# Two one-bank PSUM tiles in place of a two-bank one from the last batch on, and a planner that counts the landing between dependent transfers

## The chip, the cores and the metric

The kernel runs on one core of one Trainium2 chip. The metric is device time in microseconds of one execution, lower is better; for the kernel before three runs are given, and their median is what the prediction is about. One further execution was profiled, and all rows below come from it.

## What is computed

Attention between 2,048 tokens and a small state (8 heads of 64, four sequences of 512 tokens with 32 state rows), then two MLPs on the 2,176 rows that come out of it:

```python
def _moe_ref(x, w_in, w_out):
    h = x @ w_in                          # (2176, 512) @ (512, 2048)
    neg, pos = h <= -1.0, h >= 1.0
    g = np.where(pos, h, np.where(neg, 0.0, (h + 1.0) ** 2 / 4.0))
    return g @ w_out                      # (2048, 512)

def _moe2_ref(x, w_a, w_b, w_out):        # 512 -> 1536 -> 512
    return (x @ w_a) * (x @ w_b) @ w_out
```

The weights arrive in double precision; the result is single precision.

## The kernel before, in words

**Precision.** A matrix product in single precision is made of three matmuls on a high and a low half of each operand (`three`, L376). The halves are made by a *split* (`split`, L357): ScalarE copies the value to the rounded format (L345, the high half), VectorE subtracts it (L355, the low half).

**Fewer products.** The large products use a seven-product scheme on 2 x 2 blocks. Its products are named "1" to "7", and `sums` (L776) says what happens to each result in its PSUM bank: products 1, 5, 6 and 4 are copied out by ScalarE (`copy`, L781, an ACTIVATE `f<-bank` on L345), products 2, 3 and 7 are added by VectorE (`add`, L784). Three banks take part, x, y and z (`TO`, L797): 1, 6, 7 and 4 go to x, 2 goes to y, 5 and 3 to z. Products 3, 6, 7 and 4 add onto what the bank holds, so product 3 begins only after bank z has been copied for product 5, and product 6 only after bank x has been copied for product 1.

**Stages.** (1) Attention and the first MLP's input layer run interleaved (`phase_one`, L1250), in four batches of 16 units. A unit (`h_mm`, L721) is six matmuls of 512 columns into one bank, followed by `gate`. The first three batches take banks 0 to 3 in turn; attention takes banks 4 and 5 for scores and 6 and 7 for the rest. From unit 48 on (`SWITCH`), the last batch, units take banks 4, 5, 6, 7, 2, 3 in turn, since attention is done; its third unit, number 50, is the first on bank 6. The first products of stage 2 are mixed into this batch. (2) `b_steps` (L870) is the first MLP's output layer, in three chunks of 2 x 368, 2 x 368 and 2 x 352 tokens. Each product has four inner blocks and two column halves m; in every block six matmuls go to the first bank of a pair and six to the second (L918 to L931). Product 5 and product 3 use banks 6 and 7 as that pair (`bz`, L856); products 1, 6, 7 and 4 use banks 0 and 1 or 2 and 3; product 2 uses 4 and 5. (3) `ab_run` (L1049) makes the second MLP's two input layers and multiplies them: six pairs of inner blocks, three token chunks each; a product is six matmuls, and the rows `p` are stored to DRAM in four pieces per chunk (L1086 to L1093). Meanwhile the third weight matrix is converted and put into DRAM (`u_conv`, L1367). Conversions (`conv_steps`, L389) are a weight load (L400), a byte copy on ScalarE (L420), another ScalarE pass (L345) and a VectorE step (L433). (4) `o_plain` (L1168) and eight times `o_run` (L1185) make the output from `p`. A run loads 256 tokens of `p` in two loads (L1187), and a product is 18 matmuls of 256 columns. The first run's products 1, 5, 2, 6, 3 are followed by the second run's product 1. The buffers of the runs' loads lie where stage 3 kept its result rows, so the load of the second run waits until the last of those rows have been stored.

**PSUM tiles.** Banks 0 to 5 are six tiles of one bank each; banks 6 and 7 are the two halves of one tile of 1,024 columns (L450 to L452).

**The order.** Nothing is ordered by hand. Each operation is recorded by `Flow.op` (L46) with what it reads and writes, and `Flow.order` (L85) simulates the engines and writes the instructions in the order of the simulated starts. TensorE's order is fixed, but for a few loose attention operations. The other engines take whatever is ready first, by due time among what is ready at once. On the chip every engine, and SP's queue of transfers, works strictly in that written order. Dependences through DRAM are kept by cells of 32 columns (`GRAIN`, L27), and PSUM by bank. A transfer's landing is reckoned as the wire time of its bytes plus a latency; for all other dependences between operations of one engine the follower may start when the engine is free (L178):

```python
DMA_RATE = 390e3
DMA_LAT = 2.2
...
fin[i] = free[e] + self.LAT[e]
if ops[i][3]:
    wire = max(wire, free[e]) + ops[i][3] / self.DMA_RATE
    fin[i] = wire + self.DMA_LAT
for s in after[i]:
    left[s] -= 1
    when[s] = max(when[s], free[e] if (e,) == (*ops[s][0],) else fin[i])
```

All transfers belong to the one engine SP, so two transfers that depend on each other are such a pair. The lines that do the transfers are L333 (`load`), L336 (`store`) and L400 (weights).

Of the kernel before, what the change touches and what calls it, by code (L numbers as in the profile page):

```python
# [9 lines left out]
F32 = mybir.dt.float32  # L10
# [5 lines left out]
PSUM = bass.MemoryType.PSUM  # L16
# [3 lines left out]
class Flow:  # L20
# [64 lines left out]
    def order(self):  # L85
        ops = self.ops
        n = len(ops)
        after = [[] for _ in range(n)]
        for i, (_, _, deps, _) in enumerate(ops):
            for d in deps:  # L90
                after[d].append(i)
        least = [min(e.values()) for e, _, _, _ in ops]

        est, pe = [0.0] * n, 0.0
        for i, (e, _, deps, size) in enumerate(ops):
            t = max((est[d] for d in deps), default=0.0)
            if "PE" in e:
                t = pe = max(pe, t) + least[i]
            else:
                t += least[i] + (self.DMA_LAT + size / self.DMA_RATE if size else 0)  # L100
            est[i] = t + 0.1

        late, pe = [0.0] * n, None
        ideal, t = {}, 0.0
        for i, (e, _, _, _) in enumerate(ops):
            if "PE" in e:
                if i not in self.loose:
                    ideal[i] = t
                t += least[i]
        for i in range(n - 1, -1, -1):  # L110
            e, _, _, size = ops[i]
            lat = self.LAT[next(iter(e))]
            x = min((late[s] for s in after[i]), default=est[i] + 12.0)
            took = least[i] + lat + (self.DMA_LAT + size / self.DMA_RATE if size else 0)
            late[i] = x - took
            if i in ideal:
                late[i] = min(late[i], ideal[i])
        late = [x - self.hurry[i] for i, x in enumerate(late)]
        free = dict.fromkeys(self.LAT, 0.0)
        ready = {e: [] for e in free}  # L120
        left = [len(d) for _, _, d, _ in ops]
        when, fin, start = [0.0] * n, [0.0] * n, [None] * n
        chain = [i for i in range(n) if "PE" in ops[i][0] and i not in self.loose]
        at, lag, wire = 0, 0.0, self.DMA_FROM
        shared = {"DVE": 0.0, "POOL": 0.0}

        def offer(i):
            for e in ops[i][0]:
                if e != "PE" or i in self.loose:
                    ready[e].append(i)  # L130

        for i in range(n):
            if not left[i]:
                offer(i)
        for _ in range(n):
            best = None
            for e, f in free.items():
                x = None
                if e == "PE" and at < len(chain) and not left[chain[at]]:
                    i = chain[at]  # L140
                    x = (max(f, when[i]), 1e9, i, e)
                soon = min((max(f, when[i]) for i in ready[e]), default=0.0)
                soon += self.SOON if soon < self.EARLY else 0.0

                z = None
                for i in ready[e]:
                    t = max(f, when[i])
                    if t <= soon:
                        y = (late[i], t, i)
                        z = min(z, y) if z else y  # L150
                if z:
                    y = (z[1], z[0], z[2], e)
                    x = min(x, y) if x else y
                if x:
                    best = min(best, x) if best else x
            if best is None:

                raise RuntimeError("nothing is ready")
            t, _, i, e = best
            start[i] = t  # L160
            free[e] = t + ops[i][0][e]
            if i in self.port and e in shared:
                other = shared["POOL" if e == "DVE" else "DVE"]
                free[e] += min(max(other - t, 0.0), ops[i][0][e])
                shared[e] = free[e]
            if i in ideal:
                at += 1
                lag = max(lag, t - ideal[i])
            else:
                for x in ops[i][0]:  # L170
                    ready[x].remove(i)
# [3 lines that stand above are left out]
                fin[i] = wire + self.DMA_LAT  # L175
            for s in after[i]:
                left[s] -= 1
                when[s] = max(when[s], free[e] if (e,) == (*ops[s][0],) else fin[i])  # L178
                if not left[s]:
                    offer(s)  # L180
            self.ops[i] = (*ops[i][:4], e)
        self.start, self.fin, self.lag, self.late = start, fin, lag, late
        return sorted(range(n), key=lambda i: (start[i], i))
# [3 lines left out]
def attention_then_two_mlps(  # L187
# [14 lines left out]
    P = 128  # L202
# [13 lines left out]
    SWITCH = 48  # L216
# [18 lines left out]
    flow = Flow()  # L235
    op = flow.op
# [26 lines left out]
    class V2:  # L263
# [18 lines left out]
        @property  # L282
        def regs(self):
            a = BASE[self.arena] + self.at
            return [("S", a + 4 * self.step * i, a + 4 * (self.step * i + self.n)) for i in range(self.k)]
# [17 lines left out]
    def bank(b):  # L303
        return ("P", b, b + 1)
# [23 lines left out]
    def t_mm(n, passes=1):  # L328
        return passes * max(n / 2400 + 0.0135, 0.112)
# [30 lines left out]
        hi_of(hi, src, n, regs(src), regs(hi) + list(also))  # L360
        tt(lo, src, lambda: hi(F32), ALU.subtract, n, regs(src, hi), regs(lo))

    def mms(b, cols, pairs, first, last, n, rd, onto=False, off=0):


        def emit(e):
            o = banks[b][:, off : off + cols]
            for k, (w, x) in enumerate(pairs()):

                nc.tensor.matmul(  # L370
                    o, w, x, start=first and k == 0, stop=last and k == n - 1, skip_group_check=onto
                )

        return op({"PE": n * t_mm(cols)}, emit, rd, [bank(b)])

    def three(w, x):  # L376

# [67 lines left out]
    ps = ctx.enter_context(tc.tile_pool(name="ps", bufs=1, space=PSUM))  # L445
# [2 lines left out]
    arenas["R0"] = pc.tile([P, RLO // 4], F32R, name="r0")  # L448
    arenas["F0"] = pc.tile([P, F0 // 4], F32, name="f0")
    banks = [ps.tile([P, 512], F32, name=f"bank{b}") for b in range(6)]  # L450
    upper = ps.tile([P, 1024], F32, name="bank67")
    banks += [upper[:, :512], upper[:, 512:]]  # L452
    spare = pc.tile([P, 1], F32, name="spare")
    g_d = pd.tile([F1, P, T], F32, name="g_d")
    x2_d = pd.tile([4, P, T], F32, name="x2_d")
# [236 lines left out]
    four, six = Ring([0, 1, 2, 3]), Ring([4, 5, 6, 7, 2, 3] * 2 + [6, 7, 2, 3])  # L692

    begun = {}
    units, first_w = [], []

    def gate(b, g, put):
        h = lambda: banks[b]
# [22 lines left out]
    def h_mm(j, f, cs=range(2)):  # L721
        b = begun.pop((j, f)) if cs[0] else (four if 16 * j + f < SWITCH else six)()
        n, o = divmod(f, 4)

        def pairs():
            out = []
            for q in cs:
                out += three([v()[:, P * o : P * o + P] for v in wsum[n][q]], [v() for v in att[2 * j + q]])
            return out

        used = [v.sub(P * o, P) for q in cs for v in wsum[n][q]] + [v for q in cs for v in att[2 * j + q]]
        units.append(mms(b, 512, pairs, cs[0] == 0, cs[-1] == 1, 3 * len(cs), regs(*used)))
        if cs[-1] < 1:
            begun[j, f] = b
            return
        g = (qring if 16 * j + f < SWITCH else qlast)()
        here = [dram("G", f, S * j, S * j + S)]
        gate(b, g, lambda: store(lambda: g_d[f, :, S * j : S * j + S], g, here, 1 << 18))
# [635 lines left out]
    for fp in range(F2 // 2):  # L1374
        for c in range(3):
            more = fp + 1 < F2 // 2
            s = 2 * fp + 2
# [21 lines left out]
    cols, end = o_plain()  # L1399
# [19 lines left out]
    with tc.manual_schedule():  # L1419
        nc.vector.memset(half, 0.5)  # L1420
        nc.scalar.activation(spare, half, AF.Exp)
        make_identity(nc, ident)
        pool = tc.tile_pool(name="fs", bufs=1)
        arenas["FS"] = pool.__enter__().tile([P, FSB // 4], F32, name="fs")
        for i in order:
            if i == first_rh[0]:
                pool.__exit__(None, None, None)
                del arenas["FS"]
                high = tc.tile_pool(name="rh", bufs=1)
                arenas["RH"] = high.__enter__().tile([P, (R0 - RLO) // 4], F32R, name="rh")  # L1430
                pool = tc.tile_pool(name="f1", bufs=1)
                arenas["F1"] = pool.__enter__().tile([P, F1B // 4], F32, name="f1")
            if i == first_r1[0]:
                pool.__exit__(None, None, None)
                del arenas["F1"]
                pool = tc.tile_pool(name="r1", bufs=1)
                arenas["R1"] = pool.__enter__().tile([P, F1B // 4], F32R, name="r1")
            flow.ops[i][1](flow.ops[i][4])
        pool.__exit__(None, None, None)
        high.__exit__(None, None, None)  # L1440


# [46 lines left out]
```

## Time and profile before

| | us |
|---|---|
| three runs | 732.38, 734.49, 733.77 |
| median | 733.77 |
| the profiled execution | 731.92 |
| its span, first to last instruction | 729.8 |
| TensorE busy in the span | 703.7 |
| VectorE busy | 560.1 |
| ScalarE busy | 426.1 |
| GpSimd busy | 106.8 |

PE is TensorE's matmuls, PEld its weight loads, DVE VectorE, ACT ScalarE, POOL GpSimd, SP the queue that issues the transfers. A row of the timeline tells start, duration, engine, line, operation, out<-in with tile names, and how many instructions it merges; in brackets stands how long the engine sat idle before it and what ended that. A row of waits tells the total of such idle time, how often it came and the longest. The chain is what ended last, followed back step by step. TensorE's granted clock was 0.998 of full speed over the span. Ends of matmuls are modelled, so their starts are the safer numbers.

### The profile page before, as it was taken

The page shows a single profiled execution, that of the slowest core. Times are in us where ns is not written, and L with a number is a line of the kernel's source. Part 1 is how long each engine was busy: PE and PEld are TensorE (multiplying, and loading weights), DVE is VectorE, ACT ScalarE, POOL GpSimd, SP SyncE. Part 2 cuts the span into 40 slices and gives each one's busy share as a digit, 9 for nine tenths or more (in the row PEclk, how much of TensorE's full clock was granted, in tenths as well). Part 3 has the DMA queues.
Part 4 walks back from the last instruction along what each step waited for, and adds up shares of the span by engine and source line. Part 5 has one row for each costly group of instructions (what it writes and reads, how often), then busy time and mean ns, then how long its engine had stood idle before and what let it go on. Part 6 is the DMA issues. An engine that isn't in the chain of part 4 may idle for free.

```text
span 729.8 us, 12347 instructions
## 1 busy us (share of the span) xinstructions
PE 703.7 (96%) x4818; PEld 655.8 (90%) x4818; DVE 560.1 (77%) x750; ACT 426.1 (58%) x651; POOL 106.8 (15%) x84
## 2 busy tenths in 40 slices
PE   8789999999999999999999999999999998999997
PEld 6445766889999999999999999999999998999997
DVE  6887878889897597789898786765636787986760
ACT  4887898788444445656566675655425445544440
POOL 3546676675000000000000000000000000000000
PEclk9999999999999999999999999999999999999999
DMA  9958788495666147134335757454541258354201
GB/s 346 384 187 244 263 283 277 146 343 180 221 199 234 38 134 236 50 104 170 90 127 164 261 185 244 149 177 141 186 154 40 87 158 283 102 179 138 82 37 43
DMA packets 75450, 128.92 MB, mean 177 GB/s; under 512 B 5632, under 2 KB 51200, under 8 KB 75392
## 3 DMA queue, kind: packets, MB, share of 16 engines
q1 hardware_dynamic: 75392, 128.15, 52.7%
q8 instruction: 37, 0.61, 0.4%
q14 instruction: 21, 0.17, 0.1%
HBM read 84.87 MB, written 43.25 MB: 176 GB/s over the span
## 4 chain that ended last, share of the span: by engine, by line
PE 79%; DVE 7%; DMA 6%; ACT 4%; issue 2%; POOL 1%; POOLq 0%; ACTq 0%; SPq 0%; DVEq 0%
PE bank L370 74%; DMA f<-in_w_dram 3%; PE bank L747 2%; ACT f L345 2%; DVE rh L355 1%; DMA p_d<-f 1%; DMA g_d<-fs 1%; DVE r L355 1%; PE bank L594 1%; DVE f L822 1%; DVE f L433 1%; PE bank L771 1%; DVE f L355 1%; DMA f<-p_d 1%; ACT r L345 1%
## 5 line engine op out<-in xcount | busy, mean ns | idle before, releaser
L370 PE MATMUL bank<-rh,r 128*128 128x352 f32 (+2 forms) x1398 | 224.6, 316 | 4.5 <-ACT f L345 3.8
L370 PEld LDWEIGHTS bank<-rh,r 128*128 128x128 f32 x1398 | 215.6, 189 | 7.7 <-ACT f L345 5.9
L370 PE MATMUL bank<-r,r 128*128 128x368 f32 (+1 forms) x960 | 156.6, 315 | 3.3 <-ACT f L345 3.2
L345 ACT ACTIVATE f<-bank 128x368 f32<-128x368 f32 (+3 forms) x183 | 82.3, 454 | 121.3 <-PE bank L370 120.6
L370 PEld LDWEIGHTS bank<-r,r 128*128 128x128 f32 x960 | 147.8, 188 | 4.1 <-ACT f L345 4.1
L345 ACT ACTIVATE rh<-f 128x736 fp32r<-128x736 f32 (+4 forms) x120 | 100.7, 847 | 80.8 <-PE bank L370 63.9
L355 DVE TENSOR_TENSOR rh<-f,rh 128x736 fp32r<-128x736 f32 (+5 forms) x120 | 118.3, 996 | 31.2 <-ACT rh L345 30.9
L355 DVE TENSOR_TENSOR f<-bank,f 128x368 f32<-128x368 f32 (+2 forms) x168 | 85.7, 517 | 71.3 <-PE bank L370 66.3
L370 PE MATMUL bank<-r 128*128 128x512 f32 (+1 forms) x582 | 121.7, 360 | 1.9 <-DVE r L355 1.2
L370 PEld LDWEIGHTS bank<-r 128*128 128x128 f32 x582 | 94.3, 189 | 28.9 <-issue 5.9
L355 DVE TENSOR_TENSOR r<-f,r 128x768 fp32r<-128x768 f32 (+6 forms) x85 | 95.8, 1137 | 21.4 <-ACT r L345 21.3
L345 ACT ACTIVATE r<-f 128x768 fp32r<-128x768 f32 (+6 forms) x85 | 80.3, 953 | 45.1 <-PE bank L370 18.3
L370 PE MATMUL bank<-rh 128*128 128x352 f32 (+2 forms) x564 | 93.3, 318 | 0.5 <-DVE f L355 0.5
L822 DVE TENSOR_TENSOR f<-f 128x256 f32<-128x256 f32 (+7 forms) x108 | 87.1, 824 | 5.1 <-issue 3.2
L370 PEld LDWEIGHTS bank<-rh 128*128 128x128 f32 x564 | 88.4, 189 | 1.5 <-issue 0.7
L370 PE MATMUL bank<-r,rh 128*128 128x368 f32 (+1 forms) x480 | 80.6, 315 | 0.4 <-DVE rh L355 0.4
L370 PEld LDWEIGHTS bank<-r,rh 128*128 128x128 f32 x480 | 74.2, 188 | 0.7 <-DVE rh L355 0.7
L420 ACT ACTIVATE f<-f 128x512 fp8e5<-128x512 fp8e5 (+1 forms) x31 | 32.3, 1043 | 29.7 <-DMA f<-in_w_dram 21.2
L345 ACT ACTIVATE f<-f 128x1024 fp8e5<-128x1024 f32 (+1 forms) x43 | 48.1, 1121 | 1.8 <-POOL f L422 1.6
L433 DVE SCALAR_TENSOR_TENSOR f<-f 128x1024 uint32<-128x1024 uint32 (+1 forms) x34 | 35.4, 1041 | 7.6 <-ACT f L345 7.5
L715 DVE SCALAR_TENSOR_TENSOR f<-f,bank 128x512 f32<-128x512 f32 x40 | 26.5, 680 | 8.2 <-POOL f L710 5.1
L710 POOL TENSOR_TENSOR f<-f 128x512 f32<-128x512 f32 x23 | 29.9, 1303 | 19.2 <-ACT f L701 19.0
(55 smaller groups left out, 440.8 us busy)
## 6 DMA issues: line engine op xcount, KB each, us to landing
f<-in_w_dram SPq DMA_DIRECT2D x25, 1024.0 KB, 7.1
f<-g_d SPq DMA_DIRECT2D x36, 368.0 KB, 4.7
f<-p_d SPq DMA_DIRECT2D x17, 768.0 KB, 4.8
g_d<-f SPq DMA_DIRECT2D x40, 256.0 KB, 4.6
f<-in_w_dram SPq DMA_DIRECT2D x18, 512.0 KB, 3.9
p_d<-f SPq DMA_DIRECT2D x48, 184.0 KB, 2.1
g_d<-fs SPq DMA_DIRECT2D x28, 256.0 KB, 4.9
f<-g_d SPq DMA_DIRECT2D x16, 352.0 KB, 4.5
```

Source lines behind the costliest of these rows:

```text
L345: lambda e: nc.scalar.activation(dst(), src(), func, **{k: (v() if callable(v) else v) for k, v in kws.items()}),
L355: op({"DVE": t_tt(n)}, lambda e: nc.vector.tensor_tensor(dst(), a(), b(), alu), rd, wr, port=port)
L370: nc.tensor.matmul(o, w, x, start=first and k == 0, stop=last and k == n - 1, skip_group_check=onto)
L420: nc.scalar.activation(to(), of(), AF.Copy, saturate=False)
L433: lambda e: nc.vector.scalar_tensor_tensor(out(U32), words_of(1, U32)(), 5, z(U32), ALU.logical_shift_right, ALU.bitwise_or),
L594: nc.tensor.matmul(banks[ab[q]][o : o + NS, :cols].rearrange("p (f x) -> p f x", x=P), st[q]()[64 * h : 64 * h + 64, NS * j : NS * j + NS] ...
L710: eng(e).tensor_tensor(g(), g(), g(), ALU.mult)
L715: lambda e: nc.vector.scalar_tensor_tensor(g(), g(), 1.0, h(), ALU.min, ALU.max),
L747: nc.tensor.matmul(banks[b][:, P * i : P * i + P], w[:, P * c : P * c + P], xs()[:, P * c : P * c + P], start=c == 0, stop=c == 3,)
L771: nc.tensor.matmul(banks[3][:, :128], ident, ident, start=True, stop=True)
L822: lambda e: eng(e).tensor_tensor(dst(), a(), b(), alu),
```

## The change

Three things are changed. Banks 6 and 7 stay one tile of 1,024 columns up to the last batch's third unit, the first on bank 6. There that tile's pool is closed and two tiles of one bank each take its place for the rest of the kernel. That unit is recorded as writing both banks, so it waits until both have been read. And in `Flow.order` an operation that depends on a transfer may start only when the transfer has landed, also where it is itself a transfer.

```diff
@@ Flow.order
-                when[s] = max(when[s], free[e] if (e,) == (*ops[s][0],) else fin[i])
+                when[s] = max(when[s], free[e] if (e,) == (*ops[s][0],) and not ops[i][3] else fin[i])
@@ mms
-    def mms(b, cols, pairs, first, last, n, rd, onto=False, off=0):
+    def mms(b, cols, pairs, first, last, n, rd, onto=False, off=0, also=()):
...
-        return op({"PE": n * t_mm(cols)}, emit, rd, [bank(b)])
+        return op({"PE": n * t_mm(cols)}, emit, rd, [bank(b), *also])
@@ the PSUM tiles
     banks = [ps.tile([P, 512], F32, name=f"bank{b}") for b in range(6)]
-    upper = ps.tile([P, 1024], F32, name="bank67")
-    banks += [upper[:, :512], upper[:, 512:]]
+    banks += [None] * 2
+    wide = {}
@@ h_mm
-        units.append(mms(b, 512, pairs, cs[0] == 0, cs[-1] == 1, 3 * len(cs), regs(*used)))
+        also = ()
+        if 16 * j + f == SWITCH + 2:
+            also = [("P", 6, 8)]
+            narrow.append(len(flow.ops))
+        units.append(mms(b, 512, pairs, cs[0] == 0, cs[-1] == 1, 3 * len(cs), regs(*used), also=also))
@@ where the order is written out
+        both_banks = tc.tile_pool(name="pw", bufs=1, space=PSUM)
+        opened = both_banks.__enter__()
+        for name, b in (('upper', 6),):
+            wide[name] = opened.tile([P, 1024], F32, name=name)
+            banks[b : b + 2] = [wide[name][:, :512], wide[name][:, 512:]]
...
         for i in order:
+            if i == narrow[0]:
+                both_banks.__exit__(None, None, None)
+                both_banks = tc.tile_pool(name="pn", bufs=1, space=PSUM)
+                opened = both_banks.__enter__()
+                banks[6:] = [opened.tile([P, 512], F32, name=f"bank{b}") for b in range(6, 8)]
```

## Rows read from the trace of the kernel before

**Rows 1.** The page's busy line: us, share of the span, instructions.

```profile
PE 703.7 (96%) x4818; PEld 655.8 (90%) x4818; DVE 560.1 (77%) x750; ACT 426.1 (58%) x651; POOL 106.8 (15%) x84
```

**Rows 2.** Stretches: us; busy PE, PEld, DVE, ACT, POOL; clock, DMA share, GB/s.

```profile
196.00:250.00 54.00, 54.00 (x322) 53.78 (x322) 41.87 (x45) 24.70 (x34) 0.00 (x0) 1.00 0.49 167
...
313.00:334.00 21.00, 21.00 (x131) 21.00 (x131) 19.37 (x19) 13.05 (x19) 0.00 (x0) 1.00 0.55 177
...
392.00:450.00 58.00, 57.99 (x351) 57.99 (x352) 44.51 (x71) 39.03 (x57) 0.00 (x0) 1.00 0.67 218
```

**Rows 3.** TensorE's costliest wait: waiter <- releaser, us in total, times, longest.

```profile
PE bank L370 <- ACT f L345: 7.0, 8, 3.2
```

**Rows 4.** Timeline of TensorE, stage 2, chunk 1.

```profile
235.31 8.21 PE L370 MATMUL bank<-rh 128*128 128x368 f32 x48
243.36 8.21 PE L370 MATMUL bank<-rh,r 128*128 128x368 f32 x48
252.14 1.27 PE L370 MATMUL bank<-rh,r 128*128 128x368 f32 x6 [0.57 <-ACT f L345]
253.98 6.31 PE L370 MATMUL bank<-rh,r 128*128 128x368 f32 x36 [0.57 <-ACT f L345]
```

**Rows 5.** Timeline of ScalarE, chunk 1: copies of product 5, split, of product 6.

```profile
251.61 0.48 ACT L345 ACTIVATE f<-bank 128x368 f32<-128x368 f32 x1 [1.20 <-PE bank L370]
253.45 0.48 ACT L345 ACTIVATE f<-bank 128x368 f32<-128x368 f32 x1 [1.36 <-PE bank L370]
...
263.40 0.82 ACT L345 ACTIVATE rh<-f 128x736 fp32r<-128x736 f32 x1 [1.20 <-PE bank L370]
...
268.38 0.48 ACT L345 ACTIVATE f<-bank 128x368 f32<-128x368 f32 x1 [0.18 <-PE bank L370]
269.38 0.48 ACT L345 ACTIVATE f<-bank 128x368 f32<-128x368 f32 x1 [0.53 <-PE bank L370]
```

**Rows 6.** Timeline of TensorE, stage 2, chunk 2.

```profile
304.53 5.91 PE L370 MATMUL bank<-rh,r 128*128 128x352 f32 x35 [0.60 <-DVE rh L355]
310.99 1.24 PE L370 MATMUL bank<-rh,r 128*128 128x352 f32 x6 [0.55 <-ACT f L345]
312.79 22.51 PE L370 MATMUL bank<-rh,r 128*128 128x352 f32 x138 [0.55 <-ACT f L345]
```

**Rows 7.** Timeline of TensorE, stage 4, first run: products 5, 2 and 6.

```profile
604.63 2.29 PE L370 MATMUL bank<-r,rh 128*128 128x256 f32 x18
606.75 2.29 PE L370 MATMUL bank<-r,r 128*128 128x256 f32 x18
612.25 0.97 PE L370 MATMUL bank<-r,r 128*128 128x256 f32 x6 [3.20 <-ACT f L345]
```

**Rows 8.** The chain before: start, us, what; last store, then load.

```profile
601.30 4.92 DMA p_d<-f
...
606.37 4.69 DMA f<-p_d
```

**Rows 9.** Timeline of ScalarE and VectorE there: split, copy, low half.

```profile
611.08 0.84 ACT L345 ACTIVATE r<-f 128x768 fp32r<-128x768 f32 x1 [5.04 <-DMA f<-p_d]
611.83 0.36 ACT L345 ACTIVATE f<-bank 128x256 f32<-128x256 f32 x1
611.95 0.96 DVE L355 TENSOR_TENSOR r<-f,r 128x768 fp32r<-128x768 f32 x1 [3.68 <-ACT r L345]
```

**Rows 10.** The chain before the stall at 304.53 us: its first split.

```profile
285.67 0.76 ACT rh L345
```

**Rows 11.** Timeline: last reads of banks 6 and 7; last batch's start.

```profile
137.86 1.28 DVE L355 TENSOR_TENSOR r<-bank,r 128x512 fp32r<-128x512 f32 x2
...
147.05 5.28 PE L370 MATMUL bank<-r 128*128 128x512 f32 x22
```

**Rows 12.** Timeline of ScalarE, stage 4's first split.

```profile
577.39 1.49 ACT L345 ACTIVATE r<-f 128x1536 fp32r<-128x1536 f32 x1 [1.13 <-DMA f<-p_d]
```

**Rows 13.** Waits from 392 to 585 us: conversions waiting for weight loads.

```profile
ACT f L420 <- DMA f<-in_w_dram: 7.7, 8, 1.6
```

More of the change, by code (lines that the diff above doesn't have):

```diff
@@ L694, in attention_then_two_mlps @@
     begun = {}
-    units, first_w = [], []
+    units, first_w, narrow = [], [], []
     def gate(b, g, put):
@@ L1440, in attention_then_two_mlps @@
         high.__exit__(None, None, None)
+        both_banks.__exit__(None, None, None)
 def kernel(**inputs):
```

## The prediction

> **What bounds the kernel now.** First the page's busy line: TensorE is busy 96% of the span, and no other engine is near it [rows 1]. The profiled execution took 731.92 us, its span 729.8 us, so 2.1 us lie around the span. The median of the three runs, 733.77 us, is 1.85 us above that execution; what I take off comes from the one execution, and I take it off the median. Next the stages: from 196 to 250 us and from 392 to 450 us TensorE does not pause at all [rows 2]. In such a kernel a microsecond comes back only where TensorE waits, and only if the engines that feed it have the work ready that much earlier. So the third view is the one that counts: who ended TensorE's waits. Its costliest line is one kind, matmuls waiting for ScalarE copies of a bank, 7.0 us in eight waits, the longest 3.2 us [rows 3]. Six are pairs of about 0.55 us, one pair in each of the three token chunks of the second stage (chunks 1 and 2 in [rows 4, 6]; chunk 0 has the same pair, six waits in all). One is the 3.2 us at 612 us [rows 7]. The eighth, in the last run, is on a bank of the lower six, where the change alters nothing, so I leave it.
>
> **The six waits: the PSUM half.** In each chunk product 5 ends with six matmuls into bank 6, then six into bank 7; ScalarE copies both banks; product 3 then adds onto bank 6, then bank 7. Bank 6 is complete one group before bank 7, so its copy could run beside the six matmuls into bank 7. The trace shows that it does not. The two copies start at 251.61 and 253.45 us, 1.84 us apart, each after the whole of TensorE's work so far [rows 5], and after each TensorE waits 0.57 us [rows 4]. For comparison: after product 6 the banks 2 and 3 are copied, and product 7 adds onto both at once, the same pattern on two tiles of one bank each. Those copies start at 268.38 and 269.38 us, 1.00 us apart [rows 5], and the timeline has no wait of TensorE there. I read the difference as the two-bank tile: a copy out of one half waits for the matmuls into the other.
>
> The idle column gives 4 x 0.57 + 2 x 0.55 = 3.4 us. Matmul ends are modelled, so I price by starts instead. An undisturbed block of 48 matmuls takes 243.36 - 235.31 = 8.05 us, six take 1.01 [rows 4]. The block at 243.36 us is followed at 252.14, after 8.78 us: 0.73 lost. The six at 252.14 are followed at 253.98, after 1.84 us: 0.83 lost. That is 1.56 us a chunk; chunk 2, with 352 columns, has 1.80 us between its two starts [rows 6] against 0.96 (1.01 x 352 / 368), 0.84 lost, and I give its first wait chunk 1's 0.73. Together 3 x 1.56 = **4.7 us**, with 3.4 us as the lower bound.
>
> The page shows 96% for matmuls and 90% for weight loads [rows 1], so the two measures of one engine differ by 6% of the span. [...] By the idle column both halves of the change could give 3.4 + 3.2 = 6.6 us, by starts 8.1 us.
>
> Once the halves are two tiles the cover is there: bank 6's copy (0.48 us) lies beside six matmuls (1.0 us), bank 7's copy beside the next six. Does TensorE keep the time? In those stretches ScalarE's splits wait for TensorE, by 1.2 us each [rows 5], so the feed moves with it. The next stall, 0.60 us at 304.53 us on VectorE splits [rows 6], goes back to a ScalarE split at 285.67 us that TensorE itself had released [rows 10], and should only move earlier.
>
> The edge that makes the batch's third unit wait for both banks, and the swap of the tiles there, I cost at nothing: the last read of those banks before the batch ends at 139.1 us (137.86 + 1.28), and TensorE starts the batch at 147.05 us with two other units ahead of the third [rows 11], so close to 8 us or more cover it. If that cover were gone, the price would be the wait itself. In the last batch proper TensorE does not wait, so the narrower tiles gain nothing there.
>
> **The 3.2 us wait: the planner half.** The old planner lets a load start, in its reckoning, when the store it depends on has been issued. At 601.30 us the last product rows are stored from a buffer that the next load overwrites; the load is really issued at 606.37 us, 4.92 us after the store began, and lands 4.69 us later [rows 8]. ScalarE's queue has that load's split ahead of the copy of bank 0, so ScalarE sits idle 5.04 us until 611.08, and the copy comes at 611.83 [rows 9]. TensorE, which needs the copied bank for product 6, starts at 612.25 us; the two products before it start 2.12 us apart, so it should have started at 606.75 + 2.12 = 608.9. Lost: **3.4 us** [rows 7].
>
> The new rule moves the planned landing later by the store's own transfer and latency: by the planner's constants 0.5 + 2.2 us, used here for order alone. The first run's copies after products 1 and 5 are ready one product apart, so the split goes behind the first copy for sure and about level with the second. Behind both, all 3.4 us come back. Between them TensorE stalls one product later instead: the second copy could not begin before the split ends near 611.8, product 3 would start at about 612.25 instead of 611.0, and 2.1 us come back. Then the data: the second run's first product is due at 608.9 + 2 x 2.12 = 613.1; its low half ends on VectorE at 611.95 + 0.96 = 612.9 [rows 9]. That fits with 0.2 us to spare, and another 0.96 us operation ahead of it on VectorE would cost 0.7 us. I take 3.0 us, nearer the upper bound because VectorE too should no longer stand behind a late load just before; bounds 0 and 3.4.
>
> What else moves: in chunks 0 and 1 of each pair of inner blocks the second store of each row shares a 32-column cell with the first (368 is not a multiple of 32), so the planner now issues it after the first one's landing. Weight loads, and the stores of the third weight matrix, can pass it on SP's queue. Nobody reads those rows before the last stage, whose first split (577.39 us [rows 12]) is needed when that stage's matmuls begin: 72 of 256 columns at 2.12 / 18 us and one product of stage 3 at 1.0 us lie before 602.5 us [rows 7], so near 593 us. The split's two halves, 1.5 us and about as much again, leave more than 10 us of cover; beyond that each microsecond would go straight to TensorE. The loads of the third weight matrix also start later in the plan; they have the same cover.
>
> **Sum.** 4.7 + 3.0 = 7.7 us: 733.77 - 7.7 = **726.1 us**.
>
> **Rivals.** *A: only the PSUM half pays.* The split stays ahead of the copies, or the second run's first product waits for its data instead. For it: the planner allows 2.7 us for a store that took 4.9, and the margin above is 0.2 us. Against: VectorE's work before it moves up too. 733.77 - 4.7 = 729.1 us. *B: the six waits are real.* Product 3 adds onto the bank that product 5 left, so it must wait for that bank's copy. The rows of banks 2 and 3 speak against it [rows 5]. If it holds, only the planner half is left: 733.77 - 3.4 = 730.4 us. [...] *C: VectorE becomes the bound.* It is busy 19.37 of 21 us from 313 to 334 us [rows 2]; what chunks 0 and 1 save (3.1 us) would come back as a longer stall at 304.53 us. 733.77 - 7.7 + 3.1 = 729.2 us. *D, slower: a weight conversion ahead of the copies.* Every later plan time shifts, and ScalarE is in order. From 392 to 585 us conversions wait eight times for weight loads, 7.7 us in all, up to 1.6 us [rows 13], today without harm, since two products (2.0 us) run between a copy and the matmuls that need it. If the new order puts a needed copy behind each, and the wait with the conversion outlasts those 2.0 us, eight times 1.6 us are added: 733.77 - 7.7 + 12.8 = 738.9 us. It decides only where the copy comes late by more than two products; nothing in the old order shows one.
>
> **How the numbers follow.** Forecast 0.62, A 0.16, B 0.06, C 0.07, D 0.06, no visible effect 0.03. What a measurement of this kernel can tell from no change is about 0.3%, 2.2 us. Forecast, A, C and most of B are faster by more than that: 0.88; the rest of B and no effect make 0.06; D 0.06. The range reaches down to 724.0 (full 8.1 us, 0.6 us more for the stall at 304.53, and runs up to a microsecond below the median) and up to 731.2 (B plus the 0.7 us between the median and the highest run). It leaves out D and no effect.
>
> **What would show it.** Right: each chunk's two copies start 1.0 us apart, and TensorE has no wait for them; at the head of the last stage the copies come before the split that waits for the load, and TensorE's gap there is under a microsecond. Wrong: the copies still 1.84 us apart (B); a wait of TensorE on a split of the second run's load (A); a stall over 0.6 us on VectorE splits near 300 us (C); new waits for ScalarE copies between 390 and 585 us, with a weight conversion just before (D).

## The result, and the profile after

The kernel after takes **723.58 us** in the median of four runs (722.84 to 725.26), the kernel before 734.13 us beside it. The ratio is 0.9859, with a 95% interval from 0.9828 to 0.9890, so 10.5 us less. I forecast 726.1 us with a range from 724.0: direction and both mechanisms are as forecast, and the time lies 0.42 us below the range. The forecast gain was 7.7 us; the question of this study is therefore where another 2.8 us came from. Of all executions on record one, of keep_busy (experiment 3), ran at a granted clock of 0.75 and took 868.16 us; no figure below includes it.

The page after, its busy line, and from the table of TensorE's waits the one kind that the forecast was about (us in total, times, longest):

```profile
PE 701.8 (97%) x4818; PEld 655.5 (91%) x4818; DVE 559.0 (77%) x750; ACT 426.8 (59%) x651; POOL 106.9 (15%) x84
```

```profile
PE bank L370 <- ACT f L345: 0.5, 1, 0.5
```

Busy times are within 2 us of those of [rows 1]; the work is the same. The 7.0 us in eight waits of [rows 3] have become 0.5 us in one, the one in the last run that the change doesn't touch. The span of the profiled execution is 721.5 us, 8.3 less than before. Both kernels issue the same 4,818 matmuls in the same order, so where the time went can be read by comparing their starts one by one; "matmul for matmul" below means that. By these starts the last matmul comes 9.4 us earlier. The span gains less because this execution takes 4.3 us from the end of its last matmul to the end of the span, where the profiled execution before, and a second one of the kernel after, take 3.3 us.

**The six waits.** ScalarE's timeline of the kernel after, chunk 1, with the two copies of product 5 and the two of product 6, and then TensorE's, same chunk:

```profile
249.10 0.48 ACT L345 ACTIVATE f<-bank 128x368 f32<-128x368 f32 x1 [0.19 <-PE bank L370]
250.11 0.48 ACT L345 ACTIVATE f<-bank 128x368 f32<-128x368 f32 x1 [0.53 <-PE bank L370]
...
265.21 0.48 ACT L345 ACTIVATE f<-bank 128x368 f32<-128x368 f32 x1 [0.18 <-PE bank L370]
266.21 0.48 ACT L345 ACTIVATE f<-bank 128x368 f32<-128x368 f32 x1 [0.53 <-PE bank L370]
```

```profile
233.80 8.21 PE L370 MATMUL bank<-rh 128*128 128x368 f32 x48
241.85 14.42 PE L370 MATMUL bank<-rh,r 128*128 128x368 f32 x85
```

Product 5's copies start 1.01 us apart, against 1.84 in [rows 5], and product 6's 1.00 us apart, as they did. TensorE's row runs on through both copies, where [rows 4] breaks twice with 0.57 us.

**The head of the last stage.** TensorE's timeline, then ScalarE's:

```profile
596.58 2.31 PE L370 MATMUL bank<-rh 128*128 128x256 f32 x18
598.73 2.29 PE L370 MATMUL bank<-r,rh 128*128 128x256 f32 x18
600.86 6.56 PE L370 MATMUL bank<-r,r 128*128 128x256 f32 x54
```

```profile
598.93 0.39 ACT L345 ACTIVATE f<-bank 128x256 f32<-128x256 f32 x1 [0.63 <-PE bank L370]
600.57 0.85 ACT L345 ACTIVATE r<-f 128x768 fp32r<-128x768 f32 x1 [1.25 <-DVE f L826]
601.32 0.37 ACT L345 ACTIVATE f<-bank 128x256 f32<-128x256 f32 x1
...
605.19 0.85 ACT L345 ACTIVATE r<-f 128x768 fp32r<-128x768 f32 x1 [2.77 <-DMA f<-p_d]
```

The split that waits for the second run's load is still late (2.77 us of idle time of ScalarE), but both copies now stand ahead of it in the queue. Nobody on TensorE waits: product 6 and the two products behind it run as one row of 54 matmuls.

### The profile page after: what moved, and what is told of

Same layout as the page of the kernel before. It is cut to its first block, busy times and chain, and to the rows that moved or that the text cites. A ratio compares the mean times of both kernels' runs of the same rounds, so it can differ in the third digit from the quotient of the medians.

```text
span 721.5 us, 12346 instructions
## 1 busy us (share of the span) xinstructions
PE 701.8 (97%) x4818; PEld 655.5 (91%) x4818; DVE 559.0 (77%) x750; ACT 426.8 (59%) x651; POOL 106.9 (15%) x84
## 4 chain that ended last, share of the span: by engine, by line
PE 91%; DVE 4%; ACT 2%; issue 1%; DMA 1%; POOL 0%; POOLq 0%; ACTq 0%; DVEq 0%
PE bank L370 84%; PE bank L751 2%; PE upper L594 2%; DMA f<-in_w_dram 1%; DVE r L355 1%; PE upper L680 1%; PE bank L775 1%; PE bank L523 1%; DVE fs L433 1%; DVE rh L355 1%; PE upper L665 1%; ACT f L345 1%; ACT r L345 1%; POOL fs L548 0%; ACT fs L701 0%
## 5 line engine op out<-in xcount | busy, mean ns | idle before, releaser
L345 ACT ACTIVATE rh<-f 128x736 fp32r<-128x736 f32 (+5 forms) x120 | 100.6, 846 | 80.1 <-PE bank L370 65.0
L355 DVE TENSOR_TENSOR rh<-f,rh 128x736 fp32r<-128x736 f32 (+5 forms) x120 | 116.6, 981 | 30.2 <-ACT rh L345 29.5
L433 DVE SCALAR_TENSOR_TENSOR f<-f 128x1024 uint32<-128x1024 uint32 (+1 forms) x34 | 37.1, 1091 | 7.6 <-ACT f L345 7.5
```

The source lines that it names most:

```text
L345: lambda e: nc.scalar.activation(dst(), src(), func, **{k: (v() if callable(v) else v) for k, v in kws.items()}),
L355: op({"DVE": t_tt(n)}, lambda e: nc.vector.tensor_tensor(dst(), a(), b(), alu), rd, wr, port=port)
L433: lambda e: nc.vector.scalar_tensor_tensor(out(U32), words_of(1, U32)(), 5, z(U32), ALU.logical_shift_right, ALU.bitwise_or),
```

## The experiments

All numbers below are medians in us with the ratio to the kernel before, run beside it on the same chip; kernels that ran beside each other are called a series.

**1. Each half alone.** psum_half is the kernel after with the planner's old line:

```diff
-                when[s] = max(when[s], free[e] if (e,) == (*ops[s][0],) and not ops[i][3] else fin[i])
+                when[s] = max(when[s], free[e] if (e,) == (*ops[s][0],) else fin[i])
```

plan_half is the kernel before with the opposite edit. Both original kernels went along.

> The PSUM tiles of the change, with the old rule of the planner. Theory 1 (two separate gains; what the result has beyond them is that the profiled execution of before was its luckiest): the six waits of 0.55 to 0.57 us at 194, 252 and 311 us go, the wait of about 3.2 us at the head of the last stage stays; 4.7 us faster than before. Theory 2 (the wait at the head of the last stage is longer in most executions than in the profiled one): the same six waits go, 4 to 5 us, and the wait that stays differs from 3.2 us.

> The planner's new rule, with the two-bank tile of before. Theory 1: the six waits stay, the one at the head of the last stage goes; 3.4 us faster than before, 3.0 to 4.0. Theory 2: more than 4.5 us faster, since the transfers that this wait stands for are slower in most executions of before.

> The kernel before, unchanged, for a second profile and more times. Theory 1: median near 734 us, and a profile whose waits of TensorE sum to what the first one showed (7.0 us on copies), so that the runs above 732 us lose their time elsewhere, in transfers or at the end. Theory 2: the wait at the head of the last stage is 4 to 6 us here, and the wait near 391 us on the weights differs from 0.42 us too.

> The changed kernel, unchanged, for a second profile. Both theories: 723 to 724 us, no wait of TensorE on copies between 150 and 700 us. Theory 2 adds: its times spread less than those of before, since no wait on a landing is left on TensorE's path.

| kernel | median | runs | ratio, 95% interval |
|---|---|---|---|
| before, beside them | 733.61 | 17 | 1 |
| before_again | 733.77 | 12 | 1.0002 [0.9988, 1.0015] |
| psum_half | 727.86 | 6 | 0.9924 [0.9904, 0.9944] |
| plan_half | 728.81 | 5 | 0.9929 [0.9912, 0.9945] |
| after_again | 723.98 | 4 | 0.9862 [0.9842, 0.9882] |

The halves do what they were said to do. In plan_half the wait of the last stage is gone and the six of stage 2 stay; in psum_half it is the other way round (of its three waits for copies 3.26 us is the one at the head, 0.47 the one in the last run, and 0.32 a new one at 574.59 us, which the kernel after doesn't have). From each one's table of TensorE's waits, plan_half first, then psum_half:

```profile
PE bank L370 <- ACT f L345: 3.8, 7, 0.6
```

```profile
PE bank L370 <- ACT f L345: 4.0, 3, 3.3
```

Rivals A and B fall with this, since each half pays by itself. But by the medians the PSUM half is worth 733.61 - 727.86 = 5.75 us and the planner half 733.61 - 728.81 = 4.8; by the ratios (each against 733.61) 5.6 and 5.2. I had 4.7 and at most 3.4. Something that the profiled execution of the kernel before didn't show goes away with the change.

**2. What the wait costs in other executions.** TensorE's timeline of psum_half shows it. The first product behind the wait, with the one behind it, takes 6.04 us, where the same 36 matmuls take 4.52 us in the execution of [rows 7]. First that execution, then psum_half:

```profile
612.25 4.52 PE L370 MATMUL bank<-r,r 128*128 128x256 f32 x36 [3.20 <-ACT f L345]
```

```profile
602.04 2.29 PE L370 MATMUL bank<-r,r 128*128 128x256 f32 x18
607.59 6.04 PE L370 MATMUL bank<-r,r 128*128 128x256 f32 x36 [3.26 <-ACT f L345]
```

So theory 3: behind the 3.3 us in which TensorE stood idle, its granted clock falls to half (0.50 of full speed in the windows below) in most executions, and the profiled one was among the few in which it didn't. Three more executions of the unchanged kernel before, and one of psum_half, were profiled to see.

> The kernel before, unchanged, for another profiled execution: the two looked at so far (spans 729.8 and 729.1 us) are shorter than the spans of nearly all its other executions (median near 731.6). Theory 3: an execution with a span near 731.6 has the same matmuls up to 612 us within half a microsecond, and behind the 3.3 us wait there a stretch of 3.4 us at half clock that costs 1.1 to 1.6 us. Theory 4: the difference lies elsewhere, in falls of the clock or in waits for loads in the first 160 us or near the weight loads at 300 to 590 us, which any kernel here has, and is no property of the wait at 612 us; then the clock behind that wait is full in this execution too.

> As for before_look1: theory 3 expects the half-clock stretch behind the wait at 612 us in an execution with a span near 731.6; theory 4 expects the extra 2 us ahead of that point.

> As for before_look1: theory 3 expects the half-clock stretch behind the wait at 612 us in an execution with a span near 731.6; theory 4 expects the extra 2 us ahead of that point.

> The PSUM half alone once more (spans 725.0 to 729.5, median 725.8; the one execution profiled had 726.7 and a half-clock stretch at 609 us). Theory 3: a stretch at half clock behind the 3.3 us wait again, or, without one, a span of 725.4 or less. Theory 4: the clock there may be either; the span goes with what lies ahead of 600 us.

TensorE behind the wait, in before_look2 (the timeline), and then the windows of that stretch, us; busy PE, PEld, DVE, ACT, POOL; clock, DMA share, GB/s:

```profile
612.66 6.05 PE L370 MATMUL bank<-r,r 128*128 128x256 f32 x36 [2.87 <-ACT f L345]
```

```profile
610.00:612.00 2.00, 0.00 (x0) 0.00 (x0) 0.00 (x0) 0.51 (x1) 0.00 (x0) 1.00 1.10 367
612.00:613.00 1.00, 0.34 (x2) 0.34 (x3) 0.63 (x1) 1.00 (x3) 0.00 (x0) 1.00 1.10 345
613.00:614.00 1.00, 1.00 (x9) 1.00 (x8) 1.00 (x2) 1.00 (x3) 0.00 (x0) 0.67 1.10 349
614.00:615.00 1.00, 1.00 (x6) 1.00 (x6) 1.00 (x3) 1.00 (x2) 0.00 (x0) 0.50 1.10 346
615.00:616.00 1.00, 1.00 (x7) 1.00 (x6) 1.00 (x2) 0.08 (x1) 0.00 (x0) 0.50 1.08 382
616.00:617.00 1.00, 1.00 (x7) 1.00 (x7) 1.00 (x2) 0.62 (x2) 0.00 (x0) 0.62 1.09 380
617.00:618.00 1.00, 1.00 (x11) 1.00 (x10) 1.00 (x2) 1.00 (x1) 0.00 (x0) 1.00 1.10 346
```

From 613 us on TensorE is busy all the time, but at a clock of 0.50 a window of one microsecond touches 6 or 7 matmuls instead of 10 or 11. All three executions have this (rows of 6.05, 6.05 and 5.91 us for the 36 matmuls), and so have all three profiled executions of psum_half; the two earlier ones of the kernel before have 4.52 us and a clock of 1.00. That makes six of eight. Matmul for matmul against the execution of [rows 7], these three lose 1.4, 1.2 and 1.6 us from the wait to 628 us, and nothing in the rest of the last stage. The waits themselves differ a little: 3.05, 2.87, 3.39 us. So theory 2, for which plan_half has the right number (more than 4.5 us), does not have the reason: the wait is not longer in other executions. Theory 3 holds as to place and size.

The granted clock of every execution, profiled or not, agrees. In the experiments 55 executions of the kernel before have it on record. Ten have a mean clock of 0.998 or more, as the one of the rows has, and take 732.6 us in the mean; the other 45 have 0.988 to 0.995 and take 734.0 us. The mean doesn't tell where in the span the clock fell.

Theory 4 is partly right too: of the spread ahead of 600 us (-0.7, 0.8 and 0.2 us against the first execution) none belongs to the wait. A part of it is another fall of the clock, near 56 us, behind a wait of TensorE of 2.57 us. The window from 55 to 60 us in the execution of the rows, without it, and in before_look1, with it:

```profile
55.00:60.00 5.00, 4.26 (x36) 2.16 (x36) 4.58 (x13) 3.06 (x8) 3.61 (x3) 1.00 0.58 171
```

```profile
55.00:60.00 5.00, 4.88 (x30) 2.11 (x31) 4.47 (x13) 2.90 (x6) 3.60 (x3) 0.66 0.26 86
```

Among the 13 undisturbed profiles of the kernels before and after, their halves, keep_busy and one_load, eight have this fall and lose 0.7 to 1.0 us between 55 and 62 us against the execution of the rows; the five without it lose nothing there. It comes with and without the change (two of five profiles of the kernel before, two of three of the kernel after and one_load), so the change doesn't take it away. before_look2, which lacks it, loses its time later, between 62 and 132 us.

The clock column of before_look2 accounts for what the fall behind the wait at the head of the last stage costs. It gives (0.33 + 0.50 + 0.50 + 0.38) / 0.50 = 3.4 us at half clock, half of which is 1.7 us, and the row is 1.53 us longer. Not every such wait is followed by matmuls at half clock: here it is six of eight.

**3. Is it the idle time that lowers the clock?** keep_busy is psum_half with TensorE at work through the wait: 13 small matmuls of the identity into bank 2, which nobody reads, written just ahead of the first run's product 6 (the profile counts each as two). The wait for the copy stays. It was run once by itself and once beside psum_half.

```diff
+    def fill(b, n):
+        for _ in range(n):
+            nc.tensor.matmul(banks[b][:, :128], ident, ident, start=True, stop=True)
...
+        sixes.append(len(flow.ops))
         product("6")
...
+            if i == sixes[0]:
+                fill(2, 13)
```

> The PSUM half alone (psum_half, 727.86), with 13 small matmuls (128 columns of the identity into bank 2, which nobody reads any more) put on TensorE's queue just ahead of the first output run's product 6, so that TensorE works through the 3.26 us wait at 608 us instead of standing idle. The wait for the copy itself stays. [...] Theory 1 (the wait costs its own length and no more; the excess is the spread between executions): nothing changes, 727.9 within half a microsecond.

> keep_busy once more, now in the same call as psum_half_pair. Theory 3 (TensorE standing idle for 3.3 us is what lets the clock fall, and the fall costs 1.4 us where it comes, in five of the seven executions looked at): the median lies 0.8 to 1.5 us below psum_half_pair. Rival (the fall at 609 us is given back later, or the small matmuls cost as much as they save): the two medians within 0.4 us.

> The PSUM half alone, as the other side of keep_busy_pair. Theory 3: 0.8 to 1.5 us above it; rival: within 0.4 us of it.

TensorE's timeline in keep_busy:

```profile
602.65 2.29 PE L370 MATMUL bank<-r,r 128*128 128x256 f32 x18
604.78 3.06 PE L774 MATMUL bank<-ident 128*128 128x128 f32 x26
608.08 4.53 PE L370 MATMUL bank<-r,r 128*128 128x256 f32 x36 [0.24 <-ACT f L345]
```

The small matmuls fill the wait, and the 36 behind it are back at 4.53 us. In the first series it gave 727.38, ratio 0.9902 [0.9883, 0.9921], which next to psum_half's 727.86 of another series left the matter open: 0.5 us less, where theory 3 asks for about 1.4. Beside psum_half it gave 727.2, ratio 0.9908 [0.9889, 0.9927], against 729.6, ratio 0.9929 [0.9906, 0.9951], for psum_half_pair: 2.4 us, more than the 0.8 to 1.5 expected, with intervals that overlap. Over both series the means of the ratios, 0.9905 and 0.99265, differ by 0.2%, 1.6 us, about as much as their intervals leave open. So in the one execution profiled the fall doesn't come when TensorE is kept at work; since two of the eight above lack it with the wait left idle, one execution alone doesn't prove it. The times speak for it and agree with 1.4 us without fixing that size.

**4. Is it that one load?** The new rule also moves stores and weight loads. one_load is the kernel after with the rule for the second run's two loads only:

```diff
+        self.landed = set()
...
-                when[s] = max(when[s], free[e] if (e,) == (*ops[s][0],) and not ops[i][3] else fin[i])
+                when[s] = max(when[s], free[e] if (e,) == (*ops[s][0],) and not (ops[i][3] and s in self.landed) else fin[i])
...
+        if t0 == pairs[1]:
+            flow.landed.update(range(len(flow.ops), len(flow.ops) + 2))
```

> The kernel after, with the new rule of the planner for the two loads of the second output run alone; every other transfer is planned by the old rule. SP's whole queue and all that lies before 602 us of the plan are then as in psum_half; about a dozen instructions of ScalarE and VectorE behind that point are ordered differently. If the planner half's gain is the wait at the head of the last stage and nothing else, the time is that of the kernel after, 724.0 within 0.7 us. If the other moved transfers (result stores, weight loads of the third matrix) brought part of it, the time is 724.9 or more, towards psum_half's 727.9.

It took 723.61 (722.59 to 723.70), ratio 0.9854 [0.9836, 0.9872], as the kernel after. The planner half is worth what the wait at the head of the last stage is worth; moving the other transfers brings nothing that can be measured, and costs nothing, as I had it.

**5. Two edits beyond the change.** fill puts small matmuls (the same helper as in experiment 3) into two waits of the first stage of the kernel after; single_all makes banks 6 and 7 one-bank tiles from the start, so that the two-bank tile and the swap are gone.

```diff
+            if i in (99, 203):
+                fill(0, {99: 7, 203: 10}[i])
```

```diff
-        for name, b in (('upper', 6),):
-            wide[name] = opened.tile([P, 1024], F32, name=name)
-            banks[b : b + 2] = [wide[name][:, :512], wide[name][:, 512:]]
+        banks[6:] = [opened.tile([P, 512], F32, name=f"bank{b}") for b in range(6, 8)]
...
-            if i == narrow[0]:
...
-                banks[6:] = [opened.tile([P, 512], F32, name=f"bank{b}") for b in range(6, 8)]
```

> The kernel after, with small matmuls of the identity into bank 0, dead at both places, in two waits of the first stage: 7 ahead of the state product at 24.8 us (1.98 us idle) and 10 ahead of the one at 55.2 us (2.57 us idle). Theory 3 in its general form (a fall of the clock to half follows idle stretches of TensorE, and costs what the slow stretch loses): the half-clock stretches near 25 and 56 us are gone, twelve matmuls at 25.8 us take 3.06 instead of 4.61 us, 722.3 to 723.0 in the median, up to 1.6 us below the kernel after. Rival (in that stage VectorE's splits set the pace, so TensorE catches up in its next wait whatever its clock): clock rows as above but no change of the time, 724.0 within half a microsecond; or 0.3 to 0.5 us more, where the small matmuls end after the wait would have.

> The kernel after, with banks 6 and 7 as one-bank tiles from the start, so without the two-bank tile in the first three batches and without the swap; the extra edge of unit 50 stays. If the two-bank tile costs anything in the first stage, where the state's products fill bank 6 and then bank 7 and ScalarE copies each, TensorE's waits there get shorter and the time falls below 723.4. I expect no difference beyond half a microsecond, 724.0, since a product there is finished as a whole before VectorE's and ScalarE's work on it is needed.

fill is a miss: 726.36 (724.18 to 731.30), ratio 0.9900 [0.9874, 0.9927], slower than the kernel after. TensorE's timeline of the kernel after at the first place, then that of fill at both places:

```profile
25.83 4.61 PE L370 MATMUL bank<-r 128*128 128x512 f32 x12
30.39 1.06 PE L523 MATMUL bank<-fs 64*32 64x512 f32 x8
```

```profile
23.30 1.83 PE L774 MATMUL bank<-ident 128*128 128x128 f32 x14
25.36 1.09 PE L594 MATMUL upper<-fs 64*32 64x512 f32 x16 [0.23 <-DVE r L355]
26.39 3.03 PE L370 MATMUL bank<-r 128*128 128x512 f32 x12
30.50 1.06 PE L523 MATMUL bank<-fs 64*32 64x512 f32 x8 [1.09 <-ACT fs L635]
...
51.58 2.39 PE L774 MATMUL bank<-ident 128*128 128x128 f32 x20
53.90 1.09 PE L594 MATMUL upper<-fs 64*32 64x512 f32 x16
57.55 0.71 PE L594 MATMUL upper<-fs 64*32 64x512 f32 x8 [2.57 <-DVE r L355]
```

At the first place the twelve matmuls take 3.03 us instead of the kernel after's 4.61, and gain nothing: the next product waits 1.09 us for ScalarE and starts at 30.50, where after starts it at 30.39. At the second place I had put them ahead of the wrong product. The one at 53.90 yields the value that VectorE splits for the one at 57.55, so the wait behind it is 2.57 us as before and that product starts 2.3 us later. The profiled execution of fill is also its slowest, 731.30 us, with a further 4.0 us lost between 65 and 76 us; the other five took 724.18 to 726.75, which agrees with the 2.3 us. A filler must stand right behind the last instruction that the waiting work depends on, not ahead of it.

single_all is the opposite miss. I expected no difference and it took **720.38** (719.67 to 721.04), ratio 0.9813 [0.9794, 0.9832]: below one_load's 0.9854 [0.9836, 0.9872] of the same series, which has the kernel after's time, and the best version of the study. Matmul for matmul it is 1.8 us ahead of the kernel after at 55 us and 2.6 to 3.0 us ahead from 132 to 147 us, and keeps that. ScalarE's and VectorE's halves of the splits of one state product (both banks merged in each row) and TensorE's products around them, first in the kernel after, then in single_all:

```profile
51.59 1.09 PE L594 MATMUL upper<-fs 64*32 64x512 f32 x16
52.78 1.08 ACT L345 ACTIVATE r<-upper 128x512 fp32r<-128x512 f32 x2 [0.80 <-PE upper L594]
53.90 1.29 DVE L355 TENSOR_TENSOR r<-upper,r 128x512 fp32r<-128x512 f32 x2 [1.35 <-ACT r L345]
55.24 1.09 PE L594 MATMUL upper<-fs 64*32 64x512 f32 x16 [2.57 <-DVE r L355]
```

```profile
50.88 1.09 PE L594 MATMUL bank<-fs 64*32 64x512 f32 x16
52.06 1.08 ACT L345 ACTIVATE r<-bank 128x512 fp32r<-128x512 f32 x2 [0.60 <-PE bank L594]
52.69 1.29 DVE L355 TENSOR_TENSOR r<-bank,r 128x512 fp32r<-128x512 f32 x2 [0.34 <-ACT r L345]
53.44 1.66 PE L594 MATMUL bank<-fs 64*32 64x512 f32 x13 [1.47 <-DVE r L355]
54.03 0.18 PEld L594 LDWEIGHTS bank<-fs 64*32 64x32 f32 x14 [0.46 <-DVE r L355]
```

ScalarE's two copies of that product run from 52.78 to 53.86 us in the kernel after, and VectorE begins when both are done; in single_all they run from 52.06 to 53.14, and VectorE begins after the first. So on the two-bank tile VectorE's work on bank 6 also waits for ScalarE's copy of bank 7: it begins 1.12 us after the first copy does, in single_all 0.63 us after it. TensorE's wait for it at that place is 1.47 us in single_all and 2.57 in the kernel after. The difference overstates the gain here: two of the sixteen matmuls start at 53.44 us, after VectorE's first subtraction, but the other fourteen load their weights at 54.03, after the second. From product to product that is 3.15 us instead of 3.65, a gain of 0.5 us; how the rest of the lead divides among the other state products was not worked out. The profiled execution of single_all has a clock of 1.000 over its span. Whether its shorter waits also spare it the fall near 56 us, one execution can't tell.

In these traces the two-bank tile makes the work on one bank wait for the work on the other in two places: a copy for matmuls in stage 2 (copies 1.84 us apart, 1.01 with one-bank tiles), and a subtraction for a copy in stage 1 (1.12 us against 0.63).

## Why the prediction was right, and where it fell short

**The six waits (4.7 us): right.** Matmul for matmul the kernel after is 0.2 us late at the end of the first stage, and 1.40, 3.07 and 4.57 us early behind the second wait of chunk 0, 1 and 2: 4.8 us in all. The price by starts was the right one; the idle column's 3.4 us would have been too low. Over more executions it is rather 5.0: from 183 to 336 us the eight profiled with one-bank tiles in stage 2 and the wide one before gain 4.0 to 5.6 us on the execution of the rows, 5.1 in the mean, and the six with the wide tile throughout 0.2 in the mean. My argument from banks 2 and 3, which carried this term, held.

**The wait at the head of the last stage (3.0 us): the term that was mis-sized.** The mechanism was right: the split is behind both copies, and the second run's first product isn't late. In the pair of profiled executions the step is 3.4 us (612.25 to 602.99 us, a gain of 9.26, where the gain just before was 5.9), the upper bound of which I took off 0.4. The larger error is in the sentence that takes the sum from the one execution off the median. It assumed that the profiled execution loses at this wait what the others lose. It doesn't: in six of eight profiled executions with this wait the clock falls behind it and 1.2 to 1.6 us go in addition. A median execution therefore had 3.4 + 1.4 = 4.8 us to give back here, and plan_half gave back 4.8. Where I wrote that the median is 1.85 us above the profiled execution, I had the sign of this in hand and did not ask what the 1.85 us were. The fall near 56 us, which the execution of the rows lacks too, may be another part of that difference, but it doesn't go away with the change.

**The sum, redone.** 4.8 to 5.0 for the PSUM half and 4.8 for the planner half are 9.6 to 9.8 of the 10.5 us. The rest, some 0.7 to 0.9 us, isn't assigned. It may be no more than the spread between series: beside the halves the whole change gave 733.61 - 723.98 = 9.6 us. Another candidate is where weights land near 390 us: the gain there changes by up to 1.1 us between executions, of whichever kernel.

**Rivals.** A and B fell with experiment 1. C did not come: the stall on VectorE's splits near 300 us is still one of 0.6 us (0.60 in [rows 6], 0.61 at 301.51 us after). D did not come: there is no wait for copies between 390 and 585 us. The cover for the unit that waits for both banks held, as the aligned starts don't move between 132 and 184 us. The upper end of my range, B's 730.4 plus 0.7, should have been 731.1.

**Where I looked away.** I wrote that the narrower tiles gain nothing in the last batch, which is true, and never asked what the wide tile cost in the three batches before. The change keeps it there; 3.2 us lay in it.

## What to carry to other kernels

In this kernel a tile was a unit of waiting: two banks in one tile made a bank's reader wait for the other bank's writer (copies 1.84 us apart instead of 1.01), and even for its other reader (1.12 us instead of 0.63). With a tile for each bank from the start the kernel took 720.38 us, where one_load, with the wide tile in the first three batches, took 723.61. So give every bank that is produced and consumed by itself a tile of its own, everywhere. And before a sum from one profiled execution is taken off a median, profile a few more executions: if the median lies above the profiled one, the difference may belong to the very wait that the change removes. Let a planner count a transfer's landing: left out, it made the wait of TensorE at the head of the last stage although every engine's own work was well ordered, and counted (plan_half) it took that wait away. The wait cost its length, 3.4 us in the execution of the rows, and in six of eight executions the 1.2 to 1.6 us that a lower clock took after it.

## What the runs showed of the hardware

A wait of TensorE of 2.9 to 3.4 us was followed in six of eight executions by a stretch at a clock of 0.50 of full speed (before_look2) that cost 1.2 to 1.6 us, and in two by none; what tells the two from the six was not found. With TensorE at work through the same wait the clock stayed at 1.00 (one execution profiled). Behind the wait near 55 us in the first stage, 2.57 us in the profiles of the kernels before and after, the clock fell in eight of 13 executions (0.66 in the mean from 55 to 60 us in before_look1), at a cost of 0.7 to 1.0 us. Near 25 us a fall behind a wait of 1.98 us (in the kernel after the clock is 0.77 from 24 to 28 us and 0.61 from 28 to 30) cost nothing, since without it the next product waited for ScalarE instead: 3.03 against 4.61 us for twelve matmuls, and the next start 0.1 us later, not earlier.
